# Linear attention with a gated MLP: the normalised output is turned on TensorE instead of by DMA transposes

## The chip, the cores and the metric

The kernel runs on one core of a Trainium2 chip. The metric is the device time of one execution in microseconds (us). The kernel before the change took 347.95 us, the median of three runs (346.04, 347.95 and 350.47). The profile that this document reads was taken in the execution of 346.04 us; its span, from the first to the last instruction, is 344.3 us.

## The reference

There are 8 batches. Each has 8 heads, a sequence of 576 rows and a head dimension of 64. The model is a linear attention whose output goes into a gated layer with a causal convolution over 5 taps:

```python
proj = einsum('bhsd,df->bhsf', x, w_phi)             # f = 128
proj = proj - max(abs(proj), axis=-1)
phi(x) = concat([exp(proj), exp(-proj)])             # 256 features
kv  = einsum('bhsf,bhsd->bhfd', phi(k), v);  z = sum_s phi(k)
x   = (phi(q) @ kv) / (phi(q) @ z + 1e-6)            # per batch 576 x 512 (8 heads x 64)
gate = sigmoid(sum over 5 taps of conv_w[tap] * x shifted by tap)
out  = (gate * (x @ w_val)) @ w_out                  # w_val, w_out: 512 x 512
```

The product `x @ w_val` and the convolution sum over features or shift along the sequence, so both want `x` with the features on the partitions and the sequence along the row. The normalised output comes out the other way round, with the sequence on the partitions. Between the two stands a transpose of 576 x 512 values per batch. That transpose is what the change is about.

## The kernel before, in words

The sequence is split by parity: 288 even and 288 odd rows (`HALF`), so that a 128-partition tile can hold two rows of one head. A batch goes through three stages, and three batches are in work at a time. In step i of the outer loop (line 573) batch i is the one called `sa`, batch i-1 `sb`, batch i-2 `sc`:

- **Features of batch i, beside the MLP of batch i-2.** `unit_kq` (line 483) projects one of five groups of K and Q rows into the PSUM tiles PK and PQA (line 234). VectorE takes the largest absolute value of each row (MK on line 255, MQB on line 297), ScalarE the two exponentials of K (KTIL, line 260), and GpSimd scales V (VT, line 275). The MLP of batch i-2 is `unit_gate` (GATE, line 435, ten matmuls per 128 features with the diagonal tap matrices), `unit_val` (VAL, line 447, and the product GV, line 452) and `unit_out` (OUTp, line 464). A helper `merge` (line 510) deals both lists out in proportion to weights written beside them: the order is kq, gate, val, gate, kq, val, gate, val, kq, gate, val, kq, out, out, kq, out.
- **Q features and K-V product of batch i, beside the normalised output of batch i-1.** `unit_qproj` (line 311) writes two PSUM tiles PQ, from which ScalarE makes four exponentials (QTIL, line 328). `unit_kv` fills KVPS (line 369). `unit_num` (line 390) makes one of five tiles of numerators and denominators (NUM, line 400); VectorE forms the reciprocal (RCP, line 407) and the product (XN, line 409, bf16). `unit_xt` then turns XN into XT, after the second, the fourth and the fifth tile (line 567). The emitted order is qproj, num 0, num 1, xt 0, kv, qproj, num 2, num 3, xt 1, kv, qtail, num 4, xt 2.

Steps 8 and 9 have no batch `sa`: in step 8 the MLP of batch 6 and then the normalised output of batch 7, in step 9 the MLP of batch 7 alone.

What sets the order of the work:

- **Engine order.** Each engine works its instructions in one order, which is fixed when the kernel is built. It follows the emitted order, but an instruction whose input is late may be put behind a later one that is ready. An instance is in the trace: in the second stage the four matmuls of line 317 run before the four of line 322, although they are emitted two and two.
- **PSUM.** [...] A new tile waits until the readers of an old one are done.
- **DMA queues.** The queue of SyncE (SP) issues, in order: the DMA transposes that bring K and Q from a bf16 copy in DRAM (lines 83 and 86), the loads of V (lines 101 and 106), the transposes XN to XT (lines 422 and 426) and the stores of the result (line 478). GpSimd's queue issues the casting loads of K, Q and the weights (lines 80, 85, 216 and 219).

In step 2 the transposes of XN of batch 0 and the load of Q of batch 2 meet in SP's queue, while the two weight matrices are loaded by GpSimd's.

## Time and profile before

| what | value |
|---|---|
| median of three runs | 347.95 us |
| profiled execution | 346.04 us, span 344.3 us |
| PE (matmul) busy | 238.3 us, 69% of the span |
| ACT (ScalarE) busy | 187.6 us, 54% |
| DVE (VectorE) busy | 170.7 us, 50% |
| POOL (GpSimd) busy | 108.4 us, 31% |
| mean granted TensorE clock | 0.858 |
| DMA transposes XN to XT | 48 issues, median 2.4 us from issue to landing |
| one step in steady state (MQT to MQT, 176.79 to 211.28 us) | 34.5 us |

No engine is busy all the time, so the end is set by chains that pass from one to the other. Three views matter. The chain that ended last, followed back from the last instruction, tells which wait or instruction released which. The waits, by engine and line, tell who stood idle and what ended it. The timeline, in order of time, gives the start and the length of each instruction. In a group line, the two numbers behind the first bar are the busy time in us and the mean of one instruction in ns; behind the second bar stand the idle time just before the group's instructions and what ended most of it. "SPq" is time in which SP's queue issues a DMA, "DMA" the time of a transfer, "issue" is time in which an engine waited for nothing that the profile shows.

### The profile page before, as it was taken

How to read it: one execution, taken by the hardware profiler on the slowest of the kernel's cores; microseconds unless marked ns; L12 is line 12 of the kernel's file. 1: busy time of each engine (PE TensorE's matmuls, PEld its weight loads, DVE VectorE, ACT ScalarE, POOL GpSimd, SP SyncE). 2: the span in 40 equal slices, each digit the busy share in tenths (PEclk: the TensorE clock that was granted, in tenths of full speed). 3: DMA queues.
4: the chain of work that ended last, by engine and by line, in shares of the span. 5: the costliest groups of instructions: out<-in, count | busy, mean ns of one | idle time of the engine just before them, and what ended most of it. 6: DMA issues, size and time to landing. Idle time of an engine off the chain costs nothing.

```text
span 344.3 us, 7141 instructions
## 1 busy us (share of the span) xinstructions
PE 238.3 (69%) x2944; PEld 155.4 (45%) x2944; DVE 170.7 (50%) x253; ACT 187.6 (54%) x264; POOL 108.4 (31%) x198
## 2 busy tenths in 40 slices
PE   2467748403988498847887788769884988496494
PEld 2252525401645364434535453636362736374271
DVE  2748794501465647561856285617553765134030
ACT  2753686700468637861687368735893489123023
POOL 1153568130154127412650365034522361000000
PEclk9955766955899989996999899969996999899598
DMA  7686328997648358945596469844981026205104
GB/s 242 183 157 122 133 35 114 201 213 136 182 72 221 56 82 163 294 76 85 141 277 119 66 132 295 119 76 76 265 188 39 2 74 111 24 1 169 38 3 137
DMA packets 78779, 44.07 MB, mean 128 GB/s; under 512 B 54805, under 2 KB 70549, under 8 KB 78746
## 3 DMA queue, kind: packets, MB, share of 16 engines
q1 hardware_dynamic: 71696, 34.22, 41.3%
q0 software_dynamic: 6880, 9.31, 17.0%
q8 instruction: 23, 0.38, 0.5%
q14 instruction: 10, 0.08, 0.1%
q10 hardware_dynamic: 170, 0.08, 0.1%
HBM read 30.48 MB, written 17.69 MB: 140 GB/s over the span
## 4 chain that ended last, share of the span: by engine, by line
PE 33%; ACT 16%; DVE 16%; POOL 10%; issue 9%; SPq 7%; DMA 7%; ACTq 0%; POOLq 0%; DVEq 0%
PE GATE L435 10%; DVE MK L255 9%; POOL VT L275 8%; ACT KTIL L260 7%; ACT QTIL L328 6%; DMA XT<-XN 5%; PE VAL L447 5%; PE KVPS L369 5%; PE OUTp L464 3%; SPq L422 3%; SPq L426 2%; DVE MQB_136 L297 2%; PE KVPS L379 2%; DVE MQB_134 L297 2%; DVE GV L452 2%
## 5 line engine op out<-in xcount | busy, mean ns | idle before, releaser
L260 ACT ACTIVATE KTIL<-PK 128x1024 bf16<-128x1024 f32 (+1 forms) x80 | 70.6, 940 | 30.1 <-DVE MK L255 30.1
L435 PE MATMUL GATE<-XT,DIAG 128*128 128x288 bf16 x320 | 56.2, 327 | 39.6 <-DMA XT<-XN 32.5
L328 ACT ACTIVATE QTIL<-PQ 128x1024 bf16<-128x1024 f32 x64 | 60.7, 1027 | 11.4 <-PE PQ L322 11.4
L440 ACT ACTIVATE GS<-GATE 128x576 bf16<-128x576 f32 x32 | 20.9, 652 | 83.2 <-PE GATE L435 83.2
L452 DVE SCALAR_TENSOR_TENSOR GV<-GS,VAL 128x576 bf16<-128x576 bf16 x32 | 24.0, 750 | 70.9 <-PE VAL L447 66.2
L435 PEld LDWEIGHTS <-DIAG 128*128 128x128 bf16 x320 | 34.1, 109 | 55.3 <-issue 41.6
L255 DVE TENSOR_REDUCE MK<-PK 128x8 f32<-128x1024 f32 (+1 forms) x40 | 44.3, 1111 | 26.1 <-PE PK L234 26.1
L264 POOL TENSOR_SCALAR MK<-MK 128x8 f32<-128x8 f32 (+1 forms) x40 | 9.1, 228 | 121.6 <-DVE MK L255 121.6
L447 PE MATMUL VAL<-XT,WVAL 128*128 128x288 bf16 x256 | 41.7, 312 | 0.0
L464 PE MATMUL OUTp<-WOUT,GV 128*128 128x512 bf16 (+1 forms) x160 | 38.2, 380 | 2.0 <-ACT GS L440 1.2
L447 PEld LDWEIGHTS <-WVAL 128*128 128x128 bf16 x256 | 26.9, 107 | 10.6
L234 PE MATMUL PQA<-W_119,QT 64*128 64x128 bf16 x288 | 16.2, 235 | 21.2 <-DMA QT<-QTR_695 16.6
L297 DVE TENSOR_REDUCE MQB_134<-PQA 128x8 bf16<-128x1024 f32 (+1 forms) x20 | 21.9, 1108 | 16.9 <-PE PQA L234 16.9
L369 PE MATMUL KVPS<-VT,KTIL 128*128 128x65 bf16 x512 | 21.0, 200 | 11.8 <-ACT QTIL L328 9.4
L409 DVE TENSOR_TENSOR XN<-NUM,RCP 128x512 bf16<-128x512 f32 (+1 forms) x40 | 27.5, 689 | 1.3
L369 PEld LDWEIGHTS <-KTIL 128*128 128x128 bf16 x512 | 19.4, 102 | 16.4 <-issue 8.7
L470 ACT ACTIVATE OUTs<-OUTp 128x1024 f32<-128x1024 f32 (+1 forms) x24 | 20.9, 876 | 9.8 <-PE OUTp L464 9.7
L234 PE MATMUL PK<-W_119,KT 64*128 64x128 bf16 x288 | 16.1, 230 | 12.5 <-ACT KT L525 5.7
L464 PEld LDWEIGHTS <-GV 128*128 128x128 bf16 (+1 forms) x160 | 14.7, 100 | 20.7 <-DVE GV L452 4.3
L297 DVE TENSOR_REDUCE MQB_136<-PQA 128x8 bf16<-128x1024 f32 (+1 forms) x20 | 22.1, 1105 | 0.0
L234 PEld LDWEIGHTS <-QT 64*128 64x128 bf16 x288 | 11.0, 101 | 24.3 <-DMA QT<-QTR_695 16.8
L400 PEld LDWEIGHTS <-QTIL 128*128 128x128 bf16 x512 | 17.6, 100 | 6.8 <-issue 6.8
(196 smaller groups left out, 276.8 us busy)
## 6 DMA issues: line engine op xcount, KB each, us to landing
VN<-in_v_dram SPq DMA_DIRECT2D x16, 512.0 KB, 5.1
out_dram<-OUTs SPq DMA_DIRECT2D x24, 256.0 KB, 5.0
out_dram<-OUTs SPq DMA_DIRECT2D x8, 192.0 KB, 2.3
NKQ<-in_k_dram SPq DMA_DIRECT2D x2, 512.0 KB
NKQ<-in_q_dram SPq DMA_DIRECT2D x2, 512.0 KB, 6.7
VNt<-in_v_dram SPq DMA_DIRECT2D x16, 64.0 KB
out_dram<-OUTs SPq DMA_DIRECT2D x8, 128.0 KB, 3.6
XT<-XN SPq DMA_TRANSPOSE x48, 2.4
```

The lines of the kernel that those rows point to most:

```text
L234: nc.tensor.matmul(PS[:, par, x, :], T[ROWS[par], cols], W2[ROWS[par], :], start=True, stop=True,)
L255: nc.vector.tensor_reduce(st.MK[:, 1, sl].rearrange("p (x t) -> p t x", t=2), PK[:, :, 0:nx, :], AX.X, ALU.max, apply_absolute_value=True,)
L260: nc.scalar.activation(st.KTIL[:, sgn, sl, :].rearrange("p (x t) f -> p t x f", t=2), PK[:, :, 0:nx, :], AF.Exp, scale=1.0 - 2.0 * sgn,)
L275: st.vt_ops[u] = nc.gpsimd.tensor_tensor(st.VT[:, sgn, sl, 0:D].rearrange("p (x t) d -> p x t d", t=2), st.VN[:, 4 * hh:4 * hh + 4, 2 * jj ...
L297: nc.vector.tensor_reduce(st.MQb[:, :].rearrange("p (t s) -> p t s", t=2)[:, :, 4 * u:4 * u + n], PQ[:, :, 0:n, :], AX.X, ALU.max, apply_a ...
L328: nc.scalar.activation(st.QTIL[:, sgn, u, :, :, :], PQ[:, :, :, :], AF.Exp, scale=1.0 - 2.0 * sgn,)
L369: nc.tensor.matmul(KVPS[:, xi, c0:c0 + E1], st.KTIL[:, sgn, s, :], st.VT[:, sgn, s, :], start=(g == 0 and sgn == 0 and jp == 0), stop=Fals ...
L409: nc.vector.tensor_tensor(XN[0:m, :, :].rearrange("p (g x) d -> p g x d", g=2), NUMv[:, :, :, 0:D], RCP[0:m, :, :].unsqueeze(3).to_broadca ...
L435: nc.tensor.matmul(GATE[:, par, 0:HALF], DIAG[:, jt, tap, :], XT[:, jt, t % 2, i0:i0 + HALF], start=(tap == 0), stop=(tap == 4),)
L447: nc.tensor.matmul(VAL[:, par, 0:HALF], WVAL[:, dt, jt * P:(jt + 1) * P], XT[:, dt, par, PAD:PAD + HALF], start=(dt == 0), stop=(dt == 3),)
L452: nc.vector.scalar_tensor_tensor(out=st.GV[jt][:, :, :], in0=GS[:, :, :], scalar=1.0, in1=VAL[:, :, 0:HALF], op0=ALU.add, op1=ALU.mult,)
L464: nc.tensor.matmul(OUTp[0:m, n, :], st.GV[jt][:, :, :].rearrange("p t i -> p (t i)")[:, P * c:P * c + m], WOUT[:, jt, :], start=(jt == 0), ...
```

## The change

`unit_xt` no longer issues DMA transposes. It takes a PSUM tile XTP from the shared pool, has TensorE transpose the XN tiles into it in blocks of 128 columns against a bf16 identity that the kernel already holds, and VectorE copies the block to XT. Per batch these are 8 + 8 + 4 transposes and three copies, in place of six DMA transposes. Two sizes follow: the padding in front of each row of XT is 2 elements instead of 16, and the pool of XN tiles has 3 buffers instead of 5. Nothing else is changed; the arithmetic is the same.

```diff
-PAD = 16
+PAD = 2
...
-    xnp = ctx.enter_context(tc.tile_pool(name="xnp", bufs=5))
+    xnp = ctx.enter_context(tc.tile_pool(name="xnp", bufs=3))
...
-        nc.gpsimd.memset(st.XT[:, :, :, PAD - 2:PAD], 0.0)
+        nc.gpsimd.memset(st.XT[:, :, :, 0:PAD], 0.0)
...
     def unit_xt(st, j):
+        m = P if j < 2 else 2 * NT
+        XTP = ps2.tile([P, 4, 2, P], BF16, name="XTP", tag="b")
+        for n in range(2 if j < 2 else 1):
+            XNf = st.XN[2 * j + n][:, :, :].rearrange("p h d -> p (h d)")
+            for dt in range(4):
+                nc.tensor.transpose(
+                    XTP[:, dt, n, 0:m], XNf[0:m, dt * P:(dt + 1) * P], ident_bf[0:m, 0:m],
+                )
         i0 = PAD + P * j
         if j < 2:
-            for par in range(2):
-                XNf = st.XN[2 * j + par][:, :, :].rearrange("p h d -> p (h d)")
-                nc.sync.dma_start_transpose(st.XT[:, :, par, i0:i0 + P], XNf)
+            nc.vector.tensor_copy(st.XT[:, :, :, i0:i0 + P], XTP[:, :, :, :])
         else:
-            XNf = st.XN[4][:, :, :].rearrange("p h d -> p (h d)")
-            for par in range(2):
-                nc.sync.dma_start_transpose(st.XT[:, :, par, i0:i0 + NT], XNf[NT * par:NT * par + NT, :])
+            nc.vector.tensor_copy(
+                st.XT[:, :, :, i0:i0 + NT],
+                XTP[:, :, 0, 0:m].rearrange("p dt (t r) -> p dt t r", t=2),
+            )
```

## The prediction

> **What bounds the kernel now.** I read the chain first, then the waits, then the timeline of one steady step. The chain's shares by engine on the page show no single owner; SP's queue and DMA together hold 14% of the span. Two waits of the whole run say where:

> ```profile
> PE GATE L435 <- DMA XT<-XN: 32.5, 14, 7.0
> PE PQA L234 <- DMA QT<-QTR_695: 16.6, 1, 16.6
> ```

> The columns are the total, the number of waits and the longest. TensorE waits 32.5 us in all for transposed XN, and once 16.6 us for the Q of batch 2. The chain around one steady step (start, length, what):

> ```profile
> 187.15 0.21 DVE RCP L407
> ...
> 187.38 0.13 DVE XN L409
> ...
> 187.99 1.22 DVE MK L255
> 189.21 0.65 SPq L426
> ...
> 189.91 2.33 DMA XT<-XN
> ...
> 192.28 2.32 PE GATE L435 x9
> ```

> The last XN tile is written from 187.38 to 188.06; the gate starts in earnest at 192.28. So 4.2 us lie between, filled by SP issuing six transposes one behind the other (1.2 us each) and the last one's 2.33 us transfer. From GATE the path runs on through VAL and GATE on TensorE, so an earlier gate moves what follows.

> What TensorE's clock does meanwhile is in the windows of that step (length, busy times of PE, PEld, DVE, ACT, POOL, then granted clock, DMA share, GB/s):

> ```profile
> 190.00:191.00 1.00, 0.00 (x0) 0.00 (x0) 0.33 (x1) 1.00 (x2) 0.00 (x0) 1.00 0.13 27
> 192.00:193.00 1.00, 0.78 (x5) 0.44 (x4) 0.00 (x0) 0.00 (x0) 1.00 (x2) 0.50 0.00 0
> 196.00:197.00 1.00, 1.00 (x9) 0.64 (x7) 0.73 (x1) 0.00 (x0) 0.00 (x0) 1.00 1.13 213
> ```

> Idle from 187.67, TensorE keeps clock 1.00 until 191 and then drops to 0.50 for about three us: the first nine gate matmuls take 2.32 us, where ten later take 1.39 (195.70).

> The other place is step 2. The chain there:

> ```profile
> 65.44 1.22 DVE MK L255
> 66.66 4.27 SPq L422
> 71.03 2.64 SPq L422
> 73.76 1.22 SPq L422
> 75.15 4.27 SPq L83
> 79.51 1.19 SPq L86
> 80.79 1.19 SPq L426
> 82.03 2.40 DMA XT<-XN
> 84.47 2.34 PE GATE L435 x9
> ```

> SP issues batch 0's transposes (L422), and only then batch 2's Q (L83). TensorE has nothing from 65.1 to 81.5, then PQA, then the gate. The DMA engines are full here: their share is 1.13 to 1.32 in each 4 us window from 64 to 80, with Q, two weight matrices and V in flight. So SP's order isn't the whole cause.

> **The change, part by part.** All numbers are against the profiled execution, 346.04 us (span 344.3 plus 1.7); the median of the runs is 1.9 above it, which I add at the end.

> *Added on TensorE*: 20 transposes per batch. No bf16 run of them is in the trace. From above, 8 fp32 transposes at half clock take 1.97 us (line 135); from below, 32 NUM matmuls of 65 columns take 1.18, 37 ns apart. At 512 columns OUTp matmuls are 0.22 us apart, so 128 columns are some 55 ns by scaling, and one alone (MQT) takes 0.23. My estimate is 0.6 us for eight, 0.4 for four: 1.6 per batch; the two rows give 0.7 and 5.0 for twenty.

> *Added on VectorE*: two copies of 1024 elements and one of 256 from PSUM per batch. The nearest rows: KVSB, 520 elements, 0.70 us; MK, 1024 elements, 1.22. I take 1.2 + 1.2 + 0.43 (the slope between 512 and 1024 is 1.03 ns an element) = 2.8 us; below, 0.70 + 0.70 + 0.3 = 1.7. VectorE is busy 4.2 of 6.2 us in the window 182.3 to 188.5, so the first two copies fit, tightly.

> Source and destination of the copy are bf16. [...]

> *Second stage, steady step.* ScalarE sets its pace: eight QTIL of 0.94 us and two QTILt, 178.24 to 187.6, with breaks of 0.33 (before the second PQ pair) and 0.11. XTP 0 needs XN 0 (180.0) and XN 1 (180.8) and a PSUM buffer. TensorE stands idle at that time:

> ```profile
> 180.55 1.17 PE L369 MATMUL KVPS<-VT,KTIL 128*128 128x65 bf16 x32 [1.02 <-ACT QTIL L328]
> ```

> One half of the eight transposes fits into that 1.02 us; the other half comes behind XN 1 and delays KVPS or the second PQ pair by about 0.4 us. XTP 1 does the same to PQt. I count 0.4 for each, so NUM 4 and XN 4 come 0.8 later. If the fourfold PSUM ring hands KVPS a later buffer, it waits for the second PQ's exponentials (182.3 instead of 180.5), 1.8 more; if both halves fit into idle time, nothing: bounds 0 to 3.5 for the stage.

> *From XN 4 to the gate.* Was 4.2 us. Now: four transposes 0.4, hand-overs 0.1 (XN's and NUM's successors in the trace start 0.02 to 0.05 behind), the copy 0.43, and perhaps MK of the next features ahead of it on VectorE, in full 1.2. I take 0.8 of that, since it is ready first: 1.7. With the 0.8 from above the gate starts 4.2 - 1.7 - 0.8 = 1.7 us earlier. TensorE is then idle about 2.5 us at most, with transposes in the middle; had the clock stayed at 1.00, GATE 0 would be 1.2 us shorter. Pauses of about 1 us in the second stage (180.5) leave it at 1.00, but thin work between 43 and 45 us (0.40, then 0.16 busy) let it fall to 0.50. I count no clock gain, and keep 1.2 for the range. Per step then **-1.7** (bounds +1.0, from the ring, to -3.0), and five such steps (3 to 7): **-8.5**.

> [...]

> *Step 2.* Without XT in SP's queue the Q transposes can be issued from 65.6, when V's loads are issued, instead of 75.15: 9.5 us at most. With full DMA engines they land behind V (70.6, when VT could start) and take as before from 75.15 to 81.5, 6.3 us: about 77, 4.5 earlier. I take 5.5, since one XT transfer ahead of V goes too. Behind PQA the gate no longer waits for the tail (84.47 less 82.1): 2.3 more. Sum **-8** (bounds -2.3, if Q lands no earlier, and -11.8). Step 1 pays its own transposes, but step 2's stall takes that up.

> *Step 8.* No features beside it: XN 4 ends 294.0, gate 297.77. Now 0.8 + 0.4 + 0.43 + 0.1 = 1.7 instead of 3.8: **-2** (bounds -0.5, -3.5).

> *Step 9.* XN 4 ends 317.26, gate 323.57: 6.3 us, all SP's queue. VectorE runs all five XN in a row and now two copies between, 2.4 us; then 0.4 + 0.43 + 0.1: gate at 320.6, **-3** (bounds -1.5 with MQT-like slow transposes, -4.5 with copies of 0.70).

> *Nothing*: PAD, the memset (0.12 us on GpSimd) and fewer XN buffers. XN 3 and 4 now wait for the transposes of XN 0 and 1, which run 3 us before them (183.9 against 181); without that cover XN 3 would wait the 0.4. DMA work that goes (about 3.5 us of all 16 engines per batch: windows 182.3 to 188.5 and 188.6 to 191.1, shares 0.44 and 0.33) was otherwise idle time, except in step 2.

> **Sum**: -8.5 - 8 - 2 - 3 = -21.5 on 346.0 gives 324.5; on the median, **326**. With all lower bounds 346.0 + 5 - 2.3 - 0.5 - 1.5 = 346.7, with all upper 346.0 - 15 - 11.8 - 3.5 - 4.5 = 311.2. Neither is likely for all at once; I take 314 to 338 as this case's own range.

> **The rivals.**

> *Q is bound by the DMA engines.* For it: the shares above 1.1. Then step 2 gives 2.3 only: 326 + 5.7 = 332. Faster still; it lies in the range.

> *The wait moves into PSUM.* XTP makes 16 tiles of 13 in the second stage; KVPS already waits 9.4 us in all for QTIL, so the ring is tight. With 1 to 2 us lost in each of five steps the outer gains (-13) shrink to about -5: 343, no measurable change. Against it: six of the sixteen tiles are freed by VectorE within a us.

> *Slower: ScalarE starves.* If TensorE's fixed order puts all eight transposes of XTP 0 and 1 ahead of KVPS and PQ, each waits for XN 1 or 3 (1.3 us behind NUM: two RCP and XN pairs), runs 0.6, then KVPS waits 1.8 for the ring: 3.5 at XTP 0, 2.5 at XTP 1, where breaks of 0.33 and 0.11 are now. The last copy falls behind MK and MQB (2.4 us), so XN 4 to the gate takes 3.3 instead of 4.2: net +5 a step, +25 over five, +4 in step 8, less 8 and 3: 348 + 18 = 366. It decides from about +4 a step. Against it: in the trace an instruction whose input is late is put behind a ready one (line 322 behind 317).

> **Chances.** 326: 0.58. DMA-bound Q, 332: 0.18. PSUM, 343: 0.13. Slower, 366: 0.11. Measurement can't tell less than 2%, 7 us, from no change: faster 0.76, same 0.13, slower 0.11. For 8 in 10 the range is 313 to 342: it holds both faster cases but their edges, and half of the PSUM one.

> **What would show it.** The chain of a steady step should go XN, transposes, XT copy, GATE, with no SPq between; GATE's idle for XT should fall from 32.5 us to under 10. ScalarE's breaks in the second stage should stay under 1 us. PQA in step 2 should start at about 76. I'm wrong if QTIL waits for PQ over 2 us a step, if XT's copies queue behind MK and MQB, or if Q still arrives at 81.

## The result, and the profile after

The kernel after took **306.38 us**, the median of four runs (305.57 to 306.89); the kernel before took 347.16 us in the same comparison (346.04 to 350.47, four runs). The ratio is **0.881, 95% interval 0.874 to 0.888**. Medians are of all executions; ratios and intervals leave out the few that took over 1.5% longer than the fastest of the same kernel. The forecast was 326 us with a range from 313 to 342: the direction was right, and the gain, about 40 us, is nearly twice the 21.5 us that were summed up. The profiled execution took 306.3 us, span 304.1, against 346.04 and 344.3 before.

The page of the kernel after: first the chain's shares by engine, then two groups (busy us and mean ns of one behind the first bar, idle time and what ended it behind the second). The code has moved down by 7 lines from GATE on.

```profile
PE 43%; DVE 28%; ACT 13%; DMA 9%; issue 4%; POOL 2%; ACTq 0%
...
L442 PE MATMUL GATE<-XT,DIAG 128*128 128x288 bf16 x320 | 47.1, 296 | 0.9 <-DVE XT L430 0.9
...
L423 PE MATMUL XTP<-ident_bf,XN 128*128 128x128 bf16 (+1 forms) x160 | 15.1, 218 | 16.8 <-DVE XN L409 12.4
```

SP's queue is gone from the chain; TensorE's share has grown from 33% to 43% and VectorE's from 16% to 28%. GATE waits for XT 0.9 us in the whole run, where it waited 32.5 us; the mean of one GATE matmul fell from 327 to 296 ns though its shape is the same. That second change is the clock (mean granted clock 0.858 before, 0.906 after; windows below), which the forecast counted at nothing.

The waits of TensorE (total, number, longest) have new heads:

```profile
PE XTP L423 <- DVE XN L409: 12.4, 18, 1.0
PE PQA L234 <- DMA QT<-QTR_695: 7.4, 1, 7.4
```

What is left at the boundary and in the second stage is the transposes' wait for XN, never over 1.0 us at a time. Q of batch 2 still makes TensorE wait, 7.4 us instead of 16.6.

The chain of one steady step (start, length, what), with the same place that was shown of before:

```profile
168.37 0.21 DVE RCP L407
...
168.60 0.69 DVE XN L409
...
169.34 0.23 PE XTP L423 x2
169.67 0.26 DVE XT L430
...
169.97 1.24 DVE MK L255
```

XN 4 is ready at 169.28, the last four transposes start at 169.34, the copy runs from 169.67 to 169.97, and the gate starts at 170.01: 0.73 us where 4.2 lay before. MK, which was to be charged ahead of the copy, starts behind it at 169.97, and the chain goes on through MK and not through GATE: so it is in steps 3, 5 and 6. In steps 4 and 7 it comes from late Q into GATE, in steps 8 and 9, which have no features, from the copy into GATE. In step 4 late Q makes the gate start 0.88 us later behind MQT than in these three (13.54 us instead of 12.66), yet the step is only 0.39 us longer than 30.96: the gate has some 0.5 us of room.

The windows of this step (length, busy times of PE, PEld, DVE, ACT, POOL, then granted clock, DMA share, GB/s):

```profile
168.00:169.00 1.00, 0.33 (x11) 0.22 (x7) 0.72 (x3) 0.83 (x2) 0.00 (x0) 1.00 0.00 0
169.00:170.00 1.00, 0.66 (x20) 0.56 (x20) 0.61 (x3) 0.00 (x0) 0.00 (x0) 1.00 0.00 0
170.00:171.00 1.00, 1.00 (x11) 0.79 (x9) 1.00 (x1) 0.00 (x0) 0.00 (x0) 1.00 0.00 0
```

The clock stays at 1.00 over the boundary. TensorE has one pause there, of 1.0 us behind NUM; then the transposes and the next features' matmuls fill it up to the gate, where it stood idle for 4.0 us before. The first ten gate matmuls take 1.40 us; before, nine took 2.32.

Step 2 in the chain:

```profile
66.67 0.14 PE XTP L423
66.81 7.76 DMA QT<-QTR_695
...
74.62 0.61 PE PQA L234 x7
75.22 2.52 PE GATE L442 x10
```

SP issues Q's transposes at 66.81 instead of 75.15; they land at 74.57, and the gate starts 75.2 instead of 84.5. The clock is low here, as before: 0.50 in the window from 72 to 76 us, and ten gate matmuls take 2.5 us behind the pause of 7.4 us.

Where the 40.1 us of the span went, step by step, from the starts of MQT (the beginning of the second stage) and of the gate in both timelines (the gate is taken where its run of nine or ten matmuls starts):

| stretch | before | after | difference | forecast |
|---|---|---|---|---|
| start to the gate of step 2 | 84.47 | 75.16 | -9.3 | -8 |
| that gate to the next MQT | 20.09 | 19.88 | -0.2 | 0 |
| steps 3 to 7, MQT to gate (5) | 81.89 | 65.48 | -16.4 | -8.5 |
| steps 3 to 7, gate to next MQT (5) | 96.61 | 92.18 | -4.4 | 0 |
| step 8, MQT to gate | 14.71 | 12.66 | -2.0 | -2 |
| step 8's gate to step 9's gate | 25.80 | 20.11 | -5.7 | -3 |
| gate of step 9 to the end | 20.7 | 18.7 | -2.0 | 0 |

By my estimate from this table the clock has a part in the fourth row (4.4 us), in the sixth (1.3, worked out below) and in the last (2.0): 7.7 us together, a fifth of the whole. The large miss is in the five steady steps: 20.8 us in place of 8.5.

### The profile page after: what moved, and what is told of

Its sections match the earlier page's. It is cut to its first block, busy times and chain, and to the rows that moved or that the text cites. A ratio compares the mean times of both kernels' runs of the same rounds, so it can differ in the third digit from the quotient of the medians.

```text
span 304.1 us, 7341 instructions
## 1 busy us (share of the span) xinstructions
PE 236.5 (78%) x3104; PEld 160.1 (53%) x3104; DVE 184.5 (61%) x277; ACT 186.8 (61%) x264; POOL 108.3 (36%) x198
## 4 chain that ended last, share of the span: by engine, by line
PE 43%; DVE 28%; ACT 13%; DMA 9%; issue 4%; POOL 2%; ACTq 0%
DVE MK L255 11%; PE OUTp L471 9%; PE GATE L442 7%; ACT KTIL L260 6%; PE KVPS L369 5%; PE VAL L454 4%; ACT QTIL L328 4%; DVE GV L459 4%; DVE XN L409 3%; DVE MQB_136 L297 3%; PE XTP L423 3%; PE NUM L400 3%; DMA QT<-QTR_695 3%; DVE MQB_134 L297 3%; DMA QT<-QTR_3512 2%
## 5 line engine op out<-in xcount | busy, mean ns | idle before, releaser
L328 ACT ACTIVATE QTIL<-PQ 128x1024 bf16<-128x1024 f32 x64 | 60.4, 1031 | 14.0 <-PE PQ L322 14.0
L255 DVE TENSOR_REDUCE MK<-PK 128x8 f32<-128x1024 f32 (+1 forms) x40 | 44.4, 1114 | 22.9 <-PE PK L234 22.8
L442 PE MATMUL GATE<-XT,DIAG 128*128 128x288 bf16 x320 | 47.1, 296 | 0.9 <-DVE XT L430 0.9
L447 ACT ACTIVATE GS<-GATE 128x576 bf16<-128x576 f32 x32 | 20.9, 653 | 32.5 <-PE GATE L442 32.5
L454 PE MATMUL VAL<-XT,WVAL 128*128 128x288 bf16 x256 | 38.2, 293 | 1.0 <-DVE GV L459 1.0
L442 PEld LDWEIGHTS <-DIAG 128*128 128x128 bf16 x320 | 31.0, 100 | 11.6 <-issue 1.7
L454 PEld LDWEIGHTS <-WVAL 128*128 128x128 bf16 x256 | 25.4, 100 | 9.1 <-issue 0.9
L409 DVE TENSOR_TENSOR XN<-NUM,RCP 128x512 bf16<-128x512 f32 (+1 forms) x40 | 27.6, 689 | 1.4
L423 PE MATMUL XTP<-ident_bf,XN 128*128 128x128 bf16 (+1 forms) x160 | 15.1, 218 | 16.8 <-DVE XN L409 12.4
L234 PE MATMUL PQA<-W_119,QT 64*128 64x128 bf16 x288 | 16.5, 236 | 13.9 <-DMA QT<-QTR_695 7.4
L234 PE MATMUL PK<-W_119,KT 64*128 64x128 bf16 x288 | 16.5, 229 | 12.1 <-ACT KT L532 5.7
L471 PEld LDWEIGHTS <-GV 128*128 128x128 bf16 (+1 forms) x160 | 14.7, 100 | 20.7 <-DVE GV L459 4.6
L369 PE MATMUL KVPS<-VT,KTIL 128*128 128x65 bf16 x512 | 23.5, 201 | 2.0 <-POOL VT L289 2.0
L369 PEld LDWEIGHTS <-KTIL 128*128 128x128 bf16 x512 | 20.8, 103 | 5.0 <-issue 4.1
L407 DVE RECIPROCAL RCP<-NUM 128x8 f32<-128x8 f32 (+1 forms) x40 | 8.1, 201 | 22.2 <-PE NUM L400 22.2
```

The source lines that it names most:

```text
L234: nc.tensor.matmul(PS[:, par, x, :], T[ROWS[par], cols], W2[ROWS[par], :], start=True, stop=True,)
L255: nc.vector.tensor_reduce(st.MK[:, 1, sl].rearrange("p (x t) -> p t x", t=2), PK[:, :, 0:nx, :], AX.X, ALU.max, apply_absolute_value=True,)
L328: nc.scalar.activation(st.QTIL[:, sgn, u, :, :, :], PQ[:, :, :, :], AF.Exp, scale=1.0 - 2.0 * sgn,)
L369: nc.tensor.matmul(KVPS[:, xi, c0:c0 + E1], st.KTIL[:, sgn, s, :], st.VT[:, sgn, s, :], start=(g == 0 and sgn == 0 and jp == 0), stop=Fals ...
L409: nc.vector.tensor_tensor(XN[0:m, :, :].rearrange("p (g x) d -> p g x d", g=2), NUMv[:, :, :, 0:D], RCP[0:m, :, :].unsqueeze(3).to_broadca ...
L423: nc.tensor.transpose(XTP[:, dt, n, 0:m], XNf[0:m, dt * P:(dt + 1) * P], ident_bf[0:m, 0:m],)
```

## Experiments

The theory after the result: (a) the wait for XT disappears from the path and the clock, no longer starved, holds; the clock is worth a third or more of the gain; (b) each half of the change alone saves little, since the other half's DMA transposes still hold the gate back; (c) in step 2, the place of XT's transposes in SP's queue held back Q. The rivals: the clock follows and sets nothing; the last transfer alone was the wait; Q is bound by full DMA engines. Ratios are against the kernel before on the same chip; the intervals are 95%.

### The clock, alone, in the kernel before

Thirty matmuls of 224 columns (60 in step 9) stand ahead of the gate. They write columns that nothing reads, and need no XT.

```diff
+        if jt == 0:
+            for r in range((0, 30, 30, 30, 30, 30, 30, 60)[st.b]):
+                nc.tensor.matmul(
+                    GATE[:, 0, HALF:512], DIAG[:, 0, 0, :],
+                    DIAG[:, 0, :, :].rearrange("p t f -> p (t f)")[:, 0:512 - HALF], start=True, stop=True,
+                )
```

> The kernel before, with idle matmuls added: ahead of the first gate matmul of each step from 3 on, 30 matmuls of 224 columns (60 in step 9) write the unused columns 288 to 511 of the GATE tile from the diagonal matrices, so that TensorE is busy for some 3 us of the time in which it waits for XT. The transposes stay on the DMA queue. Clock theory: the granted clock stays at 1.00 over the gate's start, the first ten gate matmuls take 1.4 us instead of 2.7, and each of steps 3 to 8 gets 1.3 us shorter, step 9 about 2: 347 - 10 = 337, ratio 0.97. Rival, that the slow clock is hidden because ScalarE and VectorE set the pace of the stage behind it: ratio 0.995 to 1.00. If the added matmuls stand in the gate's way: above 1.00.

Measured: 344.76 us (340.99 to 349.12), ratio **0.982 (0.972 to 0.992)**. That is a gain, of 1 to 3%; the clock theory asked 3%. The timeline is that of its execution of 346.33 us (start, length, line, instruction; idle before it in brackets). In it the fillers also push the gate back (steps 3 to 7 take 180.2 us in all, 178.5 before), so only the stretch behind the gate is compared, step against step. Step 3, then step 4:

```profile
120.74 1.27 PE L441 MATMUL GATE<-XT,DIAG 128*128 128x288 bf16 x9 [0.90 <-DMA XT<-XN]
...
151.39 3.04 PE L433 MATMUL GATE<-DIAG 128*128 128x224 bf16 x30
155.49 0.30 PE L441 MATMUL GATE<-XT,DIAG 128*128 128x288 bf16 x1 [1.07 <-DMA XT<-XN]
156.83 2.32 PE L441 MATMUL GATE<-XT,DIAG 128*128 128x288 bf16 x9 [1.04 <-DMA XT<-XN]
```

The fillers bridged the wait in steps 3, 5, 7 and 8 (nine gate matmuls in 1.27 us) and ended too early in 4, 6 and 9 (2.32 us). From the nine to the next MQT it took 17.67 us in steps 3 and 5 and 17.77 in step 7, against 19.28 in step 4 and 20.54 in step 6. So a lost clock costs **1.6 to 2.9 us a step** behind the gate, inside one execution. In that the clock theory holds. Its total is not shown: the fillers held the clock in part of the steps only, and delayed the gate.

### The two halves of the change

First only XN 0 to 3 on TensorE, with the new code under `if j < 2` (the last tile goes on to the old code and keeps its two DMA transposes; the padding and buffers are those of before):

```diff
+        if j < 2:
...
+            return
         i0 = PAD + P * j
         if j < 2:
```

> Only the transposes of the first four XN tiles are on TensorE; the fifth (the tail) stays with two DMA transposes (the padding stays 16, the XN buffers 5). Theory that the last tile's way alone sets the gate: the tail still needs two issues of 1.2 us and a transfer of 2.35, 3.6 to 4.2 us from XN 4 to the gate, so a steady step gains only what SP's queue had held the transposes up beyond that (0.9 us on average) and the clock still falls; step 2 gains 7, step 9 1.5: 347 - 13 = 334, ratio 0.96. Rival, that the number of DMA issues counts (four of six are gone): two thirds of the gain of 40 us, 320, ratio 0.92.

Measured: 340.9 us (339.99 to 342.01), ratio **0.978 (0.971 to 0.986)**, less of a gain than either expectation. Then only XN 4 on TensorE, with the condition turned round (`if j == 2`):

> Only the fifth XN tile is transposed on TensorE; the first four stay with four DMA transposes per batch. Theory of the queue: SP issues the four behind the Q transposes until about 188.6 of the steady step, they land 2.35 later, so the gate starts at 190.9 instead of 192.3: 1.4 to 2.4 us per step, step 2 gains 2.3, step 9 2.4: 347 - 16 = 331, ratio 0.955. Theory that only the last tile's latency counts: the whole 3 to 4 us per step, 347 - 25 = 322, ratio 0.93 or less. Both halves together would then add to less than the whole change's 40 us under the first theory, since each leaves the other's wait in place.

Measured: 333.93 us (331.74 to 335.71), ratio **0.959 (0.951 to 0.966)**, near the queue theory's 331. The halves save 2.2% and 4.2%, together 6.3%; the whole saves 11.9%.

What the first half saves is step 2 alone: its gate starts at 78.15 instead of 84.47, and Q arrives for PQA at 74.80, as in the whole change. The five steps 3 to 7 take 178.6 us against 178.5 before: nothing. The chain of a steady step in this kernel:

```profile
182.48 1.22 DVE MK L255
183.70 0.07 SPq L444
...
183.82 2.33 DMA XT<-XN
...
186.19 2.32 PE GATE L453 x9
```

The tail's transfer through DMA stayed, and it still sets the gate. And the gate is cold: nine matmuls in 2.32 us.

In the second half the tail is on TensorE and copied at 183.63, and the gate starts at 186.45 all the same. The chain, then SP's queue (start, length, line):

```profile
183.93 0.06 DVE MK L255
183.98 2.43 DMA XT<-XN
...
186.45 2.32 PE GATE L453 x9
```

```profile
173.96 1.18 SPq L106 DMA_DIRECT2D VNt<-in_v_dram  x2
175.30 2.80 SPq L83 DMA_TRANSPOSE QT<-QTR  x1
178.19 1.19 SPq L86 DMA_TRANSPOSE QT<-QTRt  x1
179.47 5.73 SPq L440 DMA_TRANSPOSE XT<-XN  x4
```

XN 3 is written by 180.64, but SP works off V's tail, Q and then four XT transposes one behind the other until 185.2; the last lands at 186.41. In the kernel before this was hidden behind the tail's own wait. So the parts don't add: each alone leaves a transfer at the gate, and with it the cold clock. This is theory (b), shown; in step 2 the halves nearly add (6.3 and 2.1 us, against 9.3 for both).

### The place of the last copy

The last transposes and the copy are emitted behind the first K-Q feature unit instead of ahead of it:

```diff
-            if c in (1, 3, 4):
+            if c in (1, 3):
...
-            us.append((1.0, lambda u=u: unit_kq(st, u)))
+            us.append((1.0, lambda u=u: (unit_kq(st, u), unit_xt(old, 2) if old and u == 0 else None)))
```

> The changed kernel with the last transposes and their copy emitted behind the first feature group of the next step, so that on VectorE the copy stands behind MK and MQB (1.13 us each) instead of ahead of them. This is the order that the prediction charged 0.8 us for. If the place of the copy sets the gate: the gate starts 2.3 us later in each of steps 3 to 7 and the clock may fall as well (1.2 more): 306 + 11 to 17 = 317 to 323, ratio to before 0.915 to 0.93. Rival, that the features gain what the gate loses (MK 0.3 us earlier): 306 to 308, ratio 0.885.

Measured: 327.74 us (325.72 to 329.46), ratio **0.941 (0.934 to 0.948)**, 21 us more than the kernel after and above both expectations. On VectorE the copy now stands behind MK and MQB. Two steps in the timeline:

```profile
109.98 0.29 PE L423 MATMUL XTP<-ident_bf,XN 64*128 64x64 bf16 x4 [0.46 <-DVE XN L409]
112.43 2.53 PE L442 MATMUL GATE<-XT,DIAG 128*128 128x288 bf16 x10 [2.17 <-DVE XT L430]
...
220.20 1.39 PE L442 MATMUL GATE<-XT,DIAG 128*128 128x288 bf16 x10 [2.17 <-DVE XT L430]
```

Behind MQT the gate starts 2.3 to 2.9 us later than the 12.66 us of an undisturbed step in four steps and 4.4 in one (step 6, where the clock fell already in the second stage, from 208.07 to 211.48). At the gate the clock is lost in the other four. From the gate to the next MQT it takes 19.46 to 20.70 us where it is lost, 17.80 where it isn't. The same pause of 2.17 us ends once in a full and else in a half clock; the last section sets the windows of three of these steps side by side.

To part the place from the clock, the same kernel with 20 fillers ahead of the gate in steps 3 to 7:

```diff
+        if jt == 0:
+            for r in range((0, 20, 20, 20, 20, 20, 0, 0)[st.b]):
+                nc.tensor.matmul(
...
```

> The kernel with XT's last copy behind the first feature unit, and 20 filler matmuls of 224 columns ahead of the gate in steps 3 to 7 (they write gate columns that nothing reads, about 0.1 us each, and need no XT), so that TensorE isn't idle while it waits for that copy. It separates the copy's place from the clock. Clock theory: the gate still starts 2.9 us later a step (5 x 2.9 = 14.5), but the first gate matmuls and the features run at full clock again, 1.7 to 2.9 us in each of four steps: about -8 us from 327.7, so 320, ratio to before 0.918. Rival, the loss is the copy's place alone and the fillers only stand in line: 327 to 330, ratio 0.94 to 0.95.

Measured: 318.58 us (317.93 to 319.96), ratio **0.911 (0.907 to 0.916)**. A hundred matmuls more make it 9 us faster:

```profile
111.33 2.09 PE L440 MATMUL GATE<-DIAG 128*128 128x224 bf16 x20
113.56 1.39 PE L448 MATMUL GATE<-XT,DIAG 128*128 128x288 bf16 x10
```

The gate starts at the same places behind MQT as without the fillers (14.98 us in step 3, 15.56 or 15.57 in three others, 17.01 in one), but warm in all five. The stretch of steps 3 to 7 is 157.7 us in the kernel after, 176.8 with the copy late and 167.8 with the copy late and the clock held. So of the 19 us **9 are the clock** at the gate, 2.2 for each of the four losses, and 10 are the copy's place. A step then takes 33.37 us instead of 30.97, 2.4 more: of the 2.9 by which the gate is late, 0.5 come back behind it (17.80 us to the next MQT instead of 18.30), which is the gate's room. Step 6 loses 1.4 us more to the clock in its second stage with the fillers too, and the kernel after has 2.7 us of late Q in the same stretch. The two kernels differ by the fillers alone, so this is the clearest measure of what a lost clock costs.

### What the transposes cost, and who sets the second stage's pace

Each of the 20 transposes of a batch is issued twice; the second writes the same values again.

```diff
-            for dt in range(4):
+            for dt in (0, 1, 2, 3, 0, 1, 2, 3):
```

> The kernel after, with each of the 20 transposes of a batch issued twice (the second run writes the same values again). It measures what the transposes cost where they stand. Path theory: the four groups of four in the second stage and the group of the tail lie on TensorE's path and the second stage grew by 0.66 us, the boundary by 0.3, so the doubles add about 1 us for each of eight batches: +8 us on 306, 314, ratio to before 0.90. Rival, TensorE has room while it waits for ScalarE's exponentials, and only the tail's 0.25 us a batch is added: +2 us, 308, ratio 0.885.

Measured: 312.94 us (312.11 to 313.92), ratio **0.903 (0.896 to 0.910)**: the path theory. A steady step is 31.97 us instead of 30.97, and the whole 1.00 us lies between MQT and the gate (13.66 us instead of 12.66). The transposes lie on the path, at 50 ns each.

Then the three copies on ScalarE (`act_copy` in place of `nc.vector.tensor_copy`):

> The kernel after, with the three copies of XT on ScalarE instead of VectorE. Theory: ScalarE sets the pace of the second stage (eight QTIL of 0.94 us with breaks below 0.8 us), so two copies of about 1 us and one of 0.3 to 0.5 lengthen each step by 1.2 to 2.4: +6 to +14 us on 306, 312 to 320, ratio to before 0.90 to 0.92. Rival, the copies fit into ScalarE's breaks while it waits for TensorE: 306 to 308, ratio 0.88 to 0.885.

Measured: 304.29 us (303.81 to 307.41), ratio **0.873 (0.867 to 0.879)**; not to be told from the kernel after, and the theory that ScalarE sets the pace of the kernel after falls. ScalarE, in the second stage, first of the kernel after, then with the copies (start, length, line):

```profile
158.79 3.77 ACT L328 ACTIVATE QTIL<-PQ 128x1024 bf16<-128x1024 f32 x4 [0.31 <-PE PQ L322]
163.32 3.77 ACT L328 ACTIVATE QTIL<-PQ 128x1024 bf16<-128x1024 f32 x4 [0.76 <-PE PQ L322]
167.75 1.08 ACT L346 ACTIVATE QTILt<-PQt 128x512 bf16<-128x512 f32 x2 [0.65 <-PE PQt L341]
```

```profile
159.31 3.77 ACT L328 ACTIVATE QTIL<-PQ 128x1024 bf16<-128x1024 f32 x4 [0.30 <-PE PQ L322]
162.94 1.05 ACT L532 ACTIVATE XT<-XTP 128x1024 bf16<-128x1024 bf16 x1
163.84 3.82 ACT L328 ACTIVATE QTIL<-PQ 128x1024 bf16<-128x1024 f32 x4
167.47 1.11 ACT L532 ACTIVATE XT<-XTP 128x1024 bf16<-128x1024 bf16 x1
```

The second four QTIL start 4.53 us behind the first in both. ScalarE's breaks take the copies, and a step stays 31.0 to 31.4 us. A mean of 2.1 us more work a batch on ScalarE (203.5 us busy instead of 186.8) costs nothing that can be measured, while 1 us more on TensorE costs 1 us. The edit also takes 1.7 us a batch off VectorE, so a small loss on ScalarE may be hidden by that.

### The part put at nothing

The padding of 16 and five XN buffers, as before, in the kernel after:

> The kernel after, with the padding of XT at 16 columns again and five XN buffers as before, instead of 2 and 3. This is the part that the prediction put at nothing. Expected: the same time, 305 to 308, ratio to before 0.877 to 0.885. Rival, three XN buffers make XN 3 and 4 wait for the transposes of XN 0 and 1, so that five would be faster: 0.4 us a step, 303 to 304.

Measured: 305.08 us (303.31 to 306.35), ratio **0.873 (0.868 to 0.878)**. The runs overlap with those of the kernel after, and the steps are within 0.4 us of its own, up or down: nothing that these runs can tell.

### Q in step 2, and late Q in steps 4 and 7

The two weight matrices are loaded in step 0 instead of step 1, in the kernel before and in the kernel after:

```diff
+            load_wval()
+            load_wout()
...
-                if i == 1:
-                    load_wval()
-                    load_wout()
```

> The kernel before, with the two weight matrices WVAL and WOUT loaded in step 0 instead of step 1; all else as it is. It tests what held Q of batch 2 back. DMA theory: the weights share the DMA engines with V and Q in step 1, so without them the batch-0 transposes and Q land sooner; Q is issued near 70 us instead of 75.15 and lands near 76 instead of 81.5: about -5 us, ratio 0.985. Queue theory: SP's order alone sets it, XT's transposes wait for XN, and the time stays: 0 to -1 us, ratio 0.997 to 1.0.

Measured: 345.04 us (341.93 to 346.17), ratio **0.991 (0.987 to 0.995)**, a change too small to count. PQA of step 2 runs at 77.69 instead of 81.52, between the two theories. The weights now delay step 0: the second stage of step 1 begins at 56.05 instead of 52.83.

> The kernel after, with the two weight matrices loaded in step 0 instead of step 1. DMA theory: in the kernel after, PQA in step 2 still waits 7.4 us for Q, whose transfer runs from 66.8 to 74.6 with full DMA engines; without the weights it lands near 70.5: -4 us, 302, ratio to before 0.87. Rival: V and K fill the DMA engines anyway: 0 to -1 us, 306, ratio 0.88.

Measured: 303.69 us (302.97 to 304.27), ratio **0.874 (0.870 to 0.879)**. Q's chain in step 2 in this kernel:

```profile
69.52 4.25 DMA QT<-QTR
...
73.81 0.61 PE PQA L234 x8
```

From issue to landing Q takes 4.25 us instead of 7.76, with the DMA share at 0.52 and 0.40 in the two windows from 68 to 76 where it was 1.26 and 1.07. So the full DMA engines do cost 3.5 us there, but Q is issued 2.7 later, and only 0.8 remains at PQA. In the kernel before, the order of SP's queue alone is worth 6.7 us: with XN 0 to 3 off that queue PQA runs at 74.80 instead of 81.52, with the weights where they were. Both causes are real, and the queue is the larger.

Most of what this kernel gains comes from steps 4 and 7, where Q was late in the kernel after (steps 3 to 7 take 154.9 us instead of 157.7). SP's queue there, in step 7 of the kernel after:

```profile
217.35 4.11 SPq L485 DMA_DIRECT2D out_dram<-OUTs  x6
223.17 1.93 SPq L106 DMA_DIRECT2D VNt<-in_v_dram  x2
225.58 3.58 SPq L83 DMA_TRANSPOSE QT<-QTR_3512  x1
```

Behind six stores and V's tail, Q lands too late for PQA (1.07 us of wait), and with it the gate starts cold: 33.42 us for that step where others take 30.97. So the kernel has a new wait of the kind that was removed. Issuing V's tail behind Q, in every step (`load_vt` is the part of V's load that fetches the tail):

```diff
+        load_vt(states[1], states[1].q_xbars[-1])
...
+            load_vt(sn, sn.q_xbars[-1])
```

> The kernel after, with the load of V's tail issued behind Q's transposes in SP's queue instead of ahead of them. In steps 4 and 7 PQA and the gate wait for Q, about 2.2 us a step. If the place of V's tail in the queue makes Q late, these two steps shorten by up to 2.2 us each and step 2 by a little: -2 to -4 us, 303, ratio 0.873. Rival: Q is late for the K and V transposes ahead of it, or V's tail is then late for its own transpose: 306 to 310, ratio 0.88 to 0.89.

Measured: 304.54 us (302.76 to 305.81), ratio **0.876 (0.870 to 0.882)**. The gate of step 7 runs ten in 1.41 us, and steps 3 to 7 take 154.94 us instead of 157.66, with every step at 30.97 or 31.07. By the times alone the gain over the kernel after is not shown: the intervals overlap. Both together:

> The kernel after with both: weights in step 0, V's tail behind Q. If the two are independent their gains add: about -6 us, 300, ratio 0.863. If both remove the same wait (that of Q in step 2), no more than the better of the two: 302, ratio 0.87.

Measured: **301.97 us** (301.79 to 303.07), ratio **0.870 (0.865 to 0.874)**. All its runs lie below all four of the kernel after. But the two weren't compared side by side, and their intervals against the kernel before only just part (0.874 as the one's upper end and the other's lower), so the gain of some 1.3% over the kernel after is likely rather than shown. In the profiles both single edits bring steps 3 to 7 to the same 154.9 us, and so does the pair: they remove the same late Q in steps 4 and 7 there, and the pair gains 1.5 us more, ahead of step 3. Why the weights' move, which changes no transfer of steps 4 and 7, also makes Q punctual there, isn't settled: SP issues Q 1.3 and 2.0 us earlier behind MQT in those steps (the six stores ahead of it take 4.22 and 3.66 us instead of 4.47 and 4.11), and TensorE's waits were only 0.71 and 1.07 us, so little decides it.

## Why the prediction was right and wrong

**Right.** The bound: XT's way through SP's queue and Q behind it. No SPq stands in the chain of a steady step; GATE's wait fell to 0.9 us (under 10 was named); ScalarE's breaks are 0.76 and 0.65 us (under 1); PQA of step 2 starts at 74.6 (76 was named). No rival came about in full: neither the PSUM ring (the four buffers of `ps2`, line 63) nor ScalarE made a large new wait (QTIL's waits for PQ rose from 11.4 to 14.0 us in the whole run, under the 2 us a step that was named), and the DMA engines held Q back by a part only.

**Wrong about the path.** The chain was to go XN, transposes, copy, GATE, "so an earlier gate moves what follows". In the steady steps 3, 5 and 6 it goes from the copy into MK, and the gate has some 0.5 us of room. What the change takes away is the wait; what then sets the step is TensorE and VectorE in turn, in the second stage and among the features.

**Steady step, the boundary (forecast 1.7 us, measured 0.73).** The term that failed is MK ahead of the copy ("I take 0.8 of that, since it is ready first"): the copy runs first. The kernel with the copy behind MK and MQB shows what that order costs: the gate 2.9 us later. The tail's copy took 0.29 us, not 0.43; transposes and hand-overs were as said.

**Steady step, the second stage (forecast +0.8, measured +0.66).** Right in size: XN 4 ends 11.93 us behind MQT, before 11.27. But "ScalarE sets its pace", said of the stage before, doesn't hold for the stage after. With the transposes in it, TensorE is on the path: doubling them costs 1.00 us a step, giving ScalarE 2.1 us more costs none. No run tests who sets it in the kernel before.

**"I count no clock gain, and keep 1.2 for the range".** Failed, and the heaviest single step: a lost clock costs 1.6 to 2.9 us in the kernel before with fillers, 2.2 in the mean with the late copy, and 1.2 in the one step of the kernel after that loses it at the gate (step 7: 19.47 us from the gate to the next MQT, 18.30 in its neighbours). I saw the clock at 0.50 in the windows of before and took the new boundary to be nearly as idle ("about 2.5 us at most"). It has one pause of 1.0 us, and the clock stays. By the table the clock is some 7.7 us of the 40; the third that theory (a) asked isn't shown. I also priced only the first nine gate matmuls; a lost clock slows VAL behind them too (1.51 us for eight with the late copy, 0.99 with the clock held). In the table the gate-to-MQT row shows 4.4 us for five steps, less than the experiments. The likely reason, which no run isolates: before, MK started 4.3 us ahead of the gate (187.99 against 192.28), so the features were ahead; now it starts with the gate (169.97 against 170.01), and the features' chain sets the end of that stretch.

**Reference step.** The step of 34.49 us that I took had the shortest way from MQT to the gate of all five, 15.49; the mean was 16.38. The forecast's five equal terms miss 0.9 each, 4.4 together.

The five steps then: from MQT to the gate 13.79 us in the forecast (15.49 less 1.7) and 12.66 in a step without late Q, 1.13 x 5 = 5.6; the reference 4.4; gate to MQT 4.4; less 2.2 for Q late in steps 4 and 7. Sum 12.3, the whole of 20.8 less 8.5.

**Copies.** My rows gave 1.2 us for 1024 elements, from MK, an fp32 reduction. The tile's view of the kernel after:

```profile
L428 DVE COPY XT<-XTP x16: 672/691/693, 59.3 to 284.5; 128x1024 bf16<-128x1024 bf16 x16
L430 DVE COPY XT<-XTP x8: 273/292/292, 67.0 to 285.1; 128x256 bf16<-128x256 bf16 x8
```

The large copy, bf16 to bf16, takes 0.69 us: the nearest row in the trace was the wrong kind. It changed little: in the chain of steps 2 to 7 no large copy stands, and ahead of step 9's gate two do, with 0.60 us each.

**Step 2 (-8 forecast, -9.3 measured).** Q arrives at 74.6 instead of the 77 I derived: the bound by full DMA engines was real (3.5 us) but less than the 8.3 us by which Q is issued earlier. **Step 8** was right to the gate (-2.05 against -2). **Step 9** is 4.4 us earlier to its gate instead of 3, and from the gates of steps 8 and 9 to the output matmuls behind them 1.3 and 2.0 us come from the clock (10.2 and 10.9 us before, 8.9 after, for the same matmuls but one, with no features beside them). Together: steps 3 to 7 12.3, step 2 1.5, step 8 1.4, step 9 3.4, which is the undersize of 18.6 us in the span (40.1 against 21.5).

## What to carry to other kernels

When a wait ends on the path, read the clock in the windows behind it too: here a pause cut from 4.0 us to 1.0 left the following work at full clock, and that was worth 1 to 3 us a time. Follow the chain past the wait that goes, too: the next bound may lie on another engine, as MK did here. Price steps from the mean of all repeats, not from one, and a copy from a row with the same data types. Where two parts of a change stand at the same gate, do both: each alone leaves the other's transfer there.

## What the runs showed of the hardware

```profile
168.22:171.63 3.41, 2.40 (x38) 1.84 (x35) 2.83 (x5) 1.01 (x3) 0.23 (x1) 1.00 0.00 0
229.66:233.07 3.41, 1.33 (x36) 1.04 (x36) 2.74 (x5) 1.08 (x2) 0.00 (x0) 1.00 0.46 101
```

```profile
109.08:112.49 3.41, 0.78 (x21) 0.58 (x16) 3.26 (x5) 1.79 (x3) 0.23 (x1) 1.00 0.00 0
218.31:221.72 3.41, 1.52 (x13) 1.20 (x13) 1.84 (x3) 2.13 (x4) 0.98 (x2) 1.00 0.00 0
249.03:252.44 3.41, 1.92 (x50) 1.51 (x43) 3.02 (x6) 1.30 (x3) 0.16 (x1) 1.00 0.02 5
```

  TensorE is busy for 2.40, 1.33, 0.78, 1.52 and 1.92 us of 3.41, shares of 0.70, 0.39, 0.23, 0.45 and 0.56; at its end the clock stayed behind the first and the fourth and fell behind the others. The window with the late copy that kept the clock holds most of the pause and, from 220.20 on, 1.5 us of the gate's matmuls and the first of VAL's; that this is why the clock stayed is not shown, since the window of step 7 was busy for longer, 1.92 us, and lost it. In steps 3, 5 and 6 of the kernel after no stretch of 3.41 us, wherever it is laid, is busy below 0.65 (the least is 2.23 us, from 211.30), and the clock stayed at 1.00. In the kernel before with fillers, step 4, the last filler ends at 154.43 and the clock falls at 156.76, behind a window busy for 1.37 us:

```profile
153.35:156.76 3.41, 1.37 (x13) 0.92 (x10) 0.71 (x1) 1.65 (x3) 1.68 (x2) 1.00 0.19 38
```

  That is a share of 0.40. What parts the windows between 0.40 and 0.62, of which one at 0.45 and one at 0.59 kept the clock and five from 0.56 to 0.58 lost it, isn't settled here.
- A copy of 128 x 1024 bf16 from PSUM takes 0.69 us on VectorE and 1.05 on ScalarE.
- The bf16 transposes show 0.22 us each in the profile, and 20 more of them a batch, in rows of four, cost 1.00 us on the path, 50 ns each.
